# Attention and two dense blocks in one kernel: the first x block split during attention, and two units of the first dense block formed around the last head

## The chip, the cores and the metric

One core of one Trainium2 chip runs the whole program. The metric is the device time of one execution in microseconds (us), from the first to the last instruction and what the runtime puts around them. Of the kernel before three runs were taken; the median counts.

## What is computed

The reference does three things in a row, all in float32. Attention: q, k, v of 2 batches x 8 heads x 768 tokens x 64 numbers; a query sees only the keys whose nearest centroid (of 16) is its own.

```python
scores = scale * np.matmul(q, k.transpose(0, 1, 3, 2))
scores = np.where(mask, scores, -1000000000.0)
attn = np.exp(scores - scores.max(-1, keepdims=True))
attn = attn / (attn.sum(-1, keepdims=True) + 1e-09)
out = np.matmul(attn, v)          # the 8 heads side by side: x, 1536 tokens x 512
```

First dense block, with a rational gate on each number of h:

```python
h = x @ w_in                      # 512 -> 2048
g = (a[0] + a[1]*h + a[2]*h**2 + a[3]*h**3) / (1 + abs(b[0])*abs(h) + abs(b[1])*h**2 + 1e-6)
y = g @ w_out                     # 2048 -> 512
```

Second dense block: h2 = y @ w_in2 (512 to 1024), SoLU (h2 times its softmax), a layer norm, and a product with w_out2 (1024 to 512).

## The kernel before

**Attention.** The main loop (L652) goes through 96 units: head n of 16, and in it a tile t of 128 queries. For one unit, `unit_scores` (L382) forms 128 x 768 scores on PE in a pair of PSUM banks (two such pairs, tag "s", go round), `unit_max` (L399) takes the row maximum on DVE (L401), and `unit_exp` (L407) the exponential on ACT (L414). Two units make a pair; `turn_p` (L424) turns the 128 x 1536 numbers of a pair in 32 x 32 blocks on DVE (L431), one pair behind the scores. When a head is turned, `pv_step` (L434) multiplies with V on PE (L441) into four banks ("pv"), spread over the units of the next head; `pv_out` (L449) copies them out on ACT (L457, two copies: u and w). Once in two heads `pair_sums` (L463) inverts the row sums, and `pair_fin` (L498) adds u and w (L502) and scales them by the inverse sums (L516) into x. x lies in three blocks of 512 tokens, XF[0] to XF[2]; its four quarters kt are the four pairs of heads of a batch. XF[0] belongs to the first batch, which is heads 0 to 7.

**The seam.** After the loop (L688 to L706) comes, in program order: the copies of head 14's product, the turn of head 15's last pair, the sums of the last pair of heads (inverse L467, spread out by a DVE copy `rw` at L472, turned by six PE transposes into a bank pair `rbp`, L475), head 15's product with V, its two copies, `split_x(0)`, and the last `pair_fin` (on DVE). `split_x` (L635) makes of a block of x a rounded part XH (ACT, L342) and the remainder XL (POOL, L638), four quarters each: the products with float32 weights are made of three products of rounded parts (xh with wh, xl with wh, xh with wl).

**First dense block.** 48 units, one per (block of x, 128 columns of w_in). `ff_h` (L741) forms h of a unit by 12 matmuls (L752) in one of four single banks. The gate: `ff_g1` (ACT L765 t, L766 y; POOL L767 and L768 the denominator q; DVE L769, L770), `ff_g2` (ACT L776 log and L777 exponential, written over h in its bank; DVE L779 to L781, which end with the gated y), `ff_g3` (ACT L786 rounded part gh; POOL L787 remainder gl). `ff_y` (L792) multiplies with w_out by 12 matmuls (L804) into two bank pairs of tag "s". The h of a unit is formed three units ahead of its y. Beside that the weights of later units are loaded (L121, by SP) and cut into parts in the background (ACT L138, L141, L149; DVE L145; POOL L150).

The program is written as calls; a scheduler of the framework sets each engine's order from its own estimate of times, and `behind` (L527) forces one instruction behind another. Each engine then runs its own queue in order and waits on semaphores.

## Time and profile before

| | us |
|---|---|
| median of 3 runs (668.08 to 671.21) | 668.9 |
| the profiled execution | 670.29 |
| its span, first to last instruction | 668.5 |
| busy in it: PE | 608.6 |
| DVE | 507.4 |
| ACT | 436.2 |
| POOL | 375.8 |

The mean granted clock of TensorE is 0.969 of full speed. PE is the tensor engine's matmuls, PEld its weight loads, DVE the vector engine, ACT the scalar engine, POOL GpSimd, SP the engine that issues most DMAs. The busy times overlap: an engine with a high share need not be the one that sets the time at every place. Attention fills the span up to about 233 us, the first dense block most of the time up to about 533 us.

### The profile page before, as it was taken

The page shows a single profiled execution, that of the slowest core. Times are in us where ns is not written, and L with a number is a line of the kernel's source. Part 1 is how long each engine was busy: PE and PEld are TensorE (multiplying, and loading weights), DVE is VectorE, ACT ScalarE, POOL GpSimd, SP SyncE. Part 2 cuts the span into 40 slices and gives each one's busy share as a digit, 9 for nine tenths or more (in the row PEclk, how much of TensorE's full clock was granted, in tenths as well). Part 3 has the DMA queues.
Part 4 walks back from the last instruction along what each step waited for, and adds up shares of the span by engine and source line. Part 5 has one row for each costly group of instructions (what it writes and reads, how often), then busy time and mean ns, then how long its engine had stood idle before and what let it go on. Part 6 is the DMA issues. An engine that isn't in the chain of part 4 may idle for free.

```text
span 668.5 us, 13805 instructions
## 1 busy us (share of the span) xinstructions
PE 608.6 (91%) x5517; PEld 473.7 (71%) x5517; DVE 507.4 (76%) x656; ACT 436.2 (65%) x796; POOL 375.8 (56%) x347
## 2 busy tenths in 40 slices
PE   7687978888878867999999999998999999999998
PEld 3565656555655556888878888876888888888887
DVE  4789999999999737887897878899899655444360
ACT  2456666765787638979889879798685444434341
POOL 8555677656889337988798989676566100000000
PEclk8589899998999988999999999999999999999999
DMA  8966676777673204222221323223000000000001
GB/s 228 273 186 167 144 223 185 179 198 183 171 189 92 54 19 171 96 66 92 96 95 64 95 64 95 67 91 88 9 0 1 0 18 17 16 32 17 31 17 47
DMA packets 22439, 64.71 MB, mean 97 GB/s; under 512 B 4532, under 2 KB 5640, under 8 KB 22376
## 3 DMA queue, kind: packets, MB, share of 16 engines
q1 hardware_dynamic: 21944, 63.67, 33.7%
q8 instruction: 43, 0.70, 0.5%
q10 hardware_dynamic: 432, 0.17, 0.1%
q14 instruction: 20, 0.16, 0.1%
HBM read 59.16 MB, written 3.19 MB: 93 GB/s over the span
## 4 chain that ended last, share of the span: by engine, by line
PE 37%; DVE 11%; ACT 7%; issue 5%; POOL 4%; DMA 0%; DVEq 0%; ACTq 0%; SPq 0%; POOLq 0%
PE hh L895 10%; PE o L946 10%; PE y L804 8%; PE h L752 6%; DVE q L779 2%; PE lt L928 2%; DVE h L780 2%; DVE xhl L638 2%; DVE y L769 1%; POOL q L768 1%; DVE y L770 1%; ACT y L766 1%; POOL gl L787 1%; ACT h L776 1%; POOL q L767 1%
## 5 line engine op out<-in xcount | busy, mean ns | idle before, releaser
L752 PE MATMUL h<-xhl,w1h 128*128 128x512 f32 x384 | 123.7, 396 | 7.8 <-DVE y L781 5.4
L414 ACT ACTIVATE p<-s,m 128x768 f32<-128x768 f32 x96 | 86.0, 897 | 58.0 <-DVE m L401 57.8
L401 DVE TENSOR_REDUCE m<-s 128x1 f32<-128x768 f32 x96 | 88.5, 934 | 15.4 <-PE s L396 15.1
L441 PE MATMUL pv<-pt,v 32*64 32x192 f32 x3072 | 84.4, 339 | 9.6 <-ACT w L457 6.6
L752 PEld LDWEIGHTS h<-xhl,w1h 128*128 128x128 f32 x384 | 72.8, 190 | 25.5 <-DVE y L781 6.5
L431 DVE STREAM_TRANSPOSE pt<-p 128x1536 f32<-128x1536 f32 x48 | 84.5, 1762 | 0.0
L787 POOL TENSOR_TENSOR gl<-y,gh 128x512 fp32r<-128x512 f32 x48 | 69.9, 1458 | 24.4 <-ACT gh L786 24.3
L390 PE MATMUL s<-k,q 128*128 128x384 f32 x192 | 62.7, 411 | 21.6 <-ACT p L414 20.8
L441 PEld LDWEIGHTS pv<-pt,v 32*64 32x64 f32 x3072 | 57.3, 134 | 30.4 <-issue 16.1
L804 PE MATMUL y<-gl,w1h 128*128 128x512 f32 x192 | 76.0, 396 | 0.8 <-POOL gl L787 0.6
L804 PE MATMUL y<-gh,w1l 128*128 128x512 f32 x192 | 75.7, 394 | 0.0
L752 PE MATMUL h<-xhl,w1l 128*128 128x512 f32 x192 | 75.7, 395 | 0.0
L804 PE MATMUL y<-gh,w1h 128*128 128x512 f32 x192 | 70.6, 394 | 0.0
L768 POOL TENSOR_TENSOR q<-q,t 128x512 f32<-128x512 f32 x48 | 65.5, 1365 | 3.1
L390 PEld LDWEIGHTS s<-k,q 128*128 128x128 f32 x192 | 31.1, 203 | 49.0 <-ACT p L414 27.0
L767 POOL TENSOR_SCALAR q<-t,ab 128x512 f32<-128x512 f32 x48 | 40.6, 845 | 38.5 <-ACT t L765 19.4
L396 PE MATMUL s<-k,q 128*128 128x384 f32 x192 | 52.4, 357 | 2.3 <-DVE k L601 2.3
L769 DVE TENSOR_TENSOR y<-y,h 128x512 f32<-128x512 f32 x48 | 32.8, 683 | 25.9 <-ACT y L766 25.8
L776 ACT ACTIVATE h<-q,qc 128x512 f32<-128x512 f32 x48 | 33.2, 691 | 23.2 <-DVE y L770 13.2
L895 PE MATMUL hh<-vh,xhl 128*128 128x512 f32 x160 | 44.9, 396 | 0.0
L804 PEld LDWEIGHTS y<-gl,w1h 128*128 128x128 f32 x192 | 36.5, 190 | 9.8 <-POOL gl L787 1.9
L804 PEld LDWEIGHTS y<-gh,w1h 128*128 128x128 f32 x192 | 36.2, 189 | 8.5 <-ACT gh L786 0.6
(160 smaller groups left out, 1338.3 us busy)
## 6 DMA issues: line engine op xcount, KB each, us to landing
raww<-in_w SPq DMA_DIRECT2D x32, 512.0 KB, 4.0
v<-in_v SPq DMA_DIRECT2D x64, 192.0 KB, 4.9
dup<-in_qT SPq DMA_DIRECT2D x31, 192.0 KB, 3.7
dup<-in_kT SPq DMA_DIRECT2D x31, 192.0 KB, 3.8
rawv<-in_w2i SPq DMA_DIRECT2D x8, 512.0 KB, 3.6
rawv<-in_w2o SPq DMA_DIRECT2D x8, 512.0 KB, 3.6
out<-ob SPq DMA_DIRECT2D x11, 256.0 KB, 2.0
pr<-in_qT SPq DMA_DIRECT2D x7, 384.0 KB, 3.9
```

What stands on the lines that cost most here:

```text
L390: r = nc.tensor.matmul(sp[:, a, 0:384], lhsT=q1[i][:, sl], rhs=k1[i][:, a * 384:(a + 1) * 384], start=True, stop=False)
L396: last["pe"] = nc.tensor.matmul(sp[:, a, 0:384], lhsT=q2[i][:, sl], rhs=k2[i][:, a * 384:(a + 1) * 384], start=False, stop=True)
L401: last["dve"] = nc.vector.tensor_reduce(m, sp[:, :, 0:384], axis=AX.XY, op=ALU.min)
L414: last["act"] = nc.scalar.activation(out=P[n, t // 2][:, t % 2], in_=sp[:, :, 0:384], func=AF.Exp, scale=-1.0, bias=m, accum_out=rs[key][: ...
L431: r = nc.vector.transpose(PT[n][:, 2 * i:2 * i + 2].rearrange("p t k -> p (t k)"), p.rearrange("p t a k -> p (t a k)"))
L441: last["pv"] = nc.tensor.matmul(pv[n][64 * c:64 * c + 64, r, 0:192].rearrange("p (t q) -> p t q", t=NT), lhsT=vv[n][sl, j], rhs=PT[n][sl, ...
L752: r = nc.tensor.matmul(hp, lhsT=w[:, kt * 128:(kt + 1) * 128], rhs=x[:, kt], start=(i == 0), stop=(i == 11))
L768: nc.gpsimd.tensor_tensor(q, q, t, op=ALU.mult)
L787: nc.gpsimd.tensor_tensor(gl, y, gh.bitcast(F32), op=ALU.subtract)
L804: nc.tensor.matmul(o, lhsT=w[:, c], rhs=g, start=(first and i == 0), stop=(last and i == 2))
L895: last["th"] = nc.tensor.matmul(hp[:, a], lhsT=y[:, kt], rhs=w[:, 512 * a:512 * a + 512], start=(kt == 0 and e == 0), stop=(kt == 3 and e ...
L946: r = nc.tensor.matmul(op[:, 0:m], lhsT=l[:, kt], rhs=w, start=(n == 0), stop=(n == 23))
```

## The change

- `split_x(0)` is taken out of the seam and handed to the loop's plan at units 64 to 79. XHL, which held its result in the space of a turned head (tag "x"), gets a tile of its own; the space "x" is instead used by the weights of units f = 12 and 13 (`wv`).
- The pools of attention are opened in another order, with V in a pool of its own.
- `turn_p` becomes a generator. In head 15 the pair of tiles 2 and 3 is turned right after the maximum of tile 4; the last pair (tiles 4 and 5) is turned in two halves of 128 x 768.
- After the loop a bank pair of tag "s" is taken as `hb`. The h of unit 0 goes into its first bank, ahead of head 15's product with V, the h of unit 1 into its second bank, behind the six transposes to `rbp`. The transposes themselves move from ahead of head 15's product to behind it (`pair_fin`).

```diff
--- before.py
+++ after.py
@@ -104,11 +104,12 @@
     wh["l"] = ctx.enter_context(tc.tile_pool(name="wh0", bufs=1))
     asg = ExitStack()
     asp = asg.enter_context(tc.tile_pool(name="asg", bufs=1, side="right"))
+    ptp = att.enter_context(tc.tile_pool(name="ptp", bufs=1))
+    fin = att.enter_context(tc.tile_pool(name="fin", bufs=2))
+    sm = att.enter_context(tc.tile_pool(name="sm", bufs=8))
+    vp = att.enter_context(tc.tile_pool(name="vp", bufs=2))
+    pp = att.enter_context(tc.tile_pool(name="pp", bufs=2))
     qk = att.enter_context(tc.tile_pool(name="qk", bufs=2))
-    pp = att.enter_context(tc.tile_pool(name="pp", bufs=2))
-    ptp = att.enter_context(tc.tile_pool(name="ptp", bufs=1))
-    sm = att.enter_context(tc.tile_pool(name="sm", bufs=8))
-    fin = att.enter_context(tc.tile_pool(name="fin", bufs=2))
     cv[0] = att.enter_context(tc.tile_pool(name="cv", bufs=2))
 
 
@@ -159,7 +160,7 @@
 
     def w1_parts(f):
         if f in (12, 13):
-            h, l = (wv.tile([128, 1024], F32R, name=f"w1{x}{f}", tag=x) for x in "hl")
+            h, l = (wv[:, 2 * i:2 * i + 2].rearrange("p a k -> p (a k)") for i in (2 * (f - 12), 2 * (f - 12) + 1))
         else:
             h = wh["l" if f in (0, 14) else "r" if f < 5 or f == 15 else "m"].tile([128, 1024], F32R, name=f"w1h{f}", tag="h")
             l = (wl1 if NPRE < f < 12 else wl0).tile([128, 1024], F32R, name=f"w1l{f}", tag="l")
@@ -203,7 +204,7 @@
     def load_v(n):
 
         b, h = divmod(n, H)
-        t = qk.tile([128, S // 32, D], F32, name=f"v{n}", tag="v", bufs=2)
+        t = vp.tile([128, S // 32, D], F32, name=f"v{n}", tag="v", bufs=2)
         for r in range(4):
             nc.sync.dma_start(out=t[32 * r:32 * r + 32], in_=v[b, h])
         vv[n] = t
@@ -372,6 +373,8 @@
 
 
     XF = [xy.tile([128, 4, 512], F32, name=f"xf{j}", tag=f"xf{j}") for j in range(3)]
+    XHL = xy.tile([128, 8, 512], F32R, name="xhl", tag="xhl")
+    XH, XL = XHL[:, 0:4], XHL[:, 4:8]
 
     P = {}
     rs = {}
@@ -427,9 +430,14 @@
                 PT[n] = xy.tile([128, NT, S], F32, name=f"pt{n}", tag="x")
             else:
                 PT[n] = ptp.tile([128, NT, S], F32, name=f"pt{n}", tag="pt")
-        p = P.pop((n, i))
-        r = nc.vector.transpose(PT[n][:, 2 * i:2 * i + 2].rearrange("p t k -> p (t k)"), p.rearrange("p t a k -> p (t a k)"))
-        behind(r, last["dve"])
+        p = P[n, i]
+        parts = 2 if (n, i) == (B * H - 1, NT // 2 - 1) else 1
+        m = 2 // parts
+        for a in range(parts):
+            r = nc.vector.transpose(PT[n][:, 2 * i + m * a:2 * i + m * a + m].rearrange("p t k -> p (t k)"),
+                                    p[:, m * a:m * a + m].rearrange("p t a k -> p (t a k)"))
+            behind(r, last["dve"])
+            yield
 
     def pv_step(n, i):
         if i == 0:
@@ -471,9 +479,7 @@
         rw = fin.tile([128, S], F32, name="rw", tag="rb", bufs=1)
         nc.vector.tensor_copy(rw.rearrange("p (t j d) -> p j t d", t=NT, j=2), r[:, :, :, None].to_broadcast([128, 2, NT, D]))
         rb = psum2("s", "rbp")
-        for t in range(NT):
-            nc.tensor.transpose(rb[:, t // 3, t % 3 * 128:t % 3 * 128 + 128], rw[:, t * 128:t * 128 + 128], ident)
-        rsd[key] = rb
+        rsd[key] = rb, rw
 
     def sums_out(key, r, u):
 
@@ -499,6 +505,12 @@
         eng = nc.vector if key == 7 else nc.gpsimd
         b, p = divmod(key, 4)
         u, w, rb = U.pop(key), W.pop(key), rsd.pop(key)
+        if key == 7:
+            rb, rw = rb
+            for t in range(NT):
+                r = nc.tensor.transpose(rb[:, t // 3, t % 3 * 128:t % 3 * 128 + 128], rw[:, t * 128:t * 128 + 128], ident)
+                if t == 0:
+                    behind(r, last["pv"])
         eng.tensor_tensor(u, u, w, op=ALU.add)
         yield
         t0 = b * S
@@ -638,6 +650,7 @@
             el.tensor_tensor(XL[:, kt], XF[j][:, kt], XH[:, kt].bitcast(F32), op=ALU.subtract)
             yield
 
+    spread(split_x(0, nc.scalar, nc.gpsimd), 5, 64, 79)
     set1_a()
     def pv_part(n, t):
 
@@ -665,8 +678,16 @@
             load_v(n)
         sp = unit_scores(n, t)
         m = unit_max(n, t, sp)
-        if t % 2 and idx > 1:
-            turn_p(*divmod(idx // 2 - 1, NT // 2))
+        if n == B * H - 1 and t >= NT - 2:
+            if t == NT - 2:
+                for _ in turn_p(n, NT // 2 - 2):
+                    pass
+            else:
+                end = turn_p(n, NT // 2 - 1)
+                next(end)
+        elif t % 2 and idx > 1:
+            for _ in turn_p(*divmod(idx // 2 - 1, NT // 2)):
+                pass
         if idx == S1B:
             set1_b()
 
@@ -687,16 +708,27 @@
         run_plan(idx)
     for i in range(2):
         pv_out(B * H - 2, i)
-    turn_p(B * H - 1, NT // 2 - 1)
+    for _ in end:
+        pass
+    hb = psum2("s", "h01")
+
+    def h_of(hp, j, f, u):
+        w_h, w_l = w1_t[f]
+        i = 0
+        for kt in range(4):
+            for w, x in ((w_h, XH), (w_h, XL), (w_l, XH)):
+                r = nc.tensor.matmul(hp, lhsT=w[:, kt * 128:(kt + 1) * 128], rhs=x[:, kt], start=(i == 0), stop=(i == 11))
+                if i == 0 and 0 < u < 4:
+                    behind(r, last["pv"])
+                i += 1
+        return hp
+
+    h_of(hb[:, 0], 0, 0, 0)
     pair_sums(B * H // 2 - 1)
     for i in range(NS):
         pv_step(B * H - 1, i)
     for i in range(2):
         pv_out(B * H - 1, i)
-    XHL = xy.tile([128, 9, 512], F32R, name="xhl", tag="x")
-    XH, XL = XHL[:, 0:4], XHL[:, 4:8]
-    for _ in split_x(0, nc.scalar, nc.gpsimd):
-        pass
     for _ in pair_fin(B * H // 2 - 1):
         pass
     for _ in range(3):
@@ -713,7 +745,6 @@
     wh["m"] = ctx.enter_context(tc.tile_pool(name="wh1", bufs=7))
     ypp = ctx.enter_context(tc.tile_pool(name="ypp", bufs=1))
     YP = [ypp.tile([128, 4, 512], F32, name=f"yp{j}", tag=f"yp{j}") for j in range(2)]
-    wv = ctx.enter_context(tc.tile_pool(name="wv", bufs=2))
     m1 = ExitStack()
     cv[0] = m1.enter_context(tc.tile_pool(name="cv1", bufs=3))
     cw = m1.enter_context(tc.tile_pool(name="cw", bufs=2))
@@ -725,6 +756,7 @@
     nc.vector.memset(qc, 1.0 + 1e-6)
     a0, a1, a2, a3 = (coef_t[:, i:i + 1] for i in range(4))
     ff_units = [(j, f) for j in (0, 1, 2) for f in range(8)] + [(j, f) for j in (2, 1, 0) for f in range(8, 16)]
+    wv = xy.tile([128, 9, 512], F32R, name="wv", tag="x")
     bg = [w1_parts(f) for f in range(NPRE, 14)]
 
     def run_bg(k):
@@ -736,24 +768,15 @@
                 bg.pop(0)
 
     gt = {}
-    hb = [None]
 
     def ff_h(u):
         j, f = ff_units[u]
-        xh, xl = XH, XL
-        w_h, w_l = w1_t[f]
         if u and u % 8 == 0 and (f == 0 or j < 2):
             for _ in split_x(j, nc.scalar, nc.vector):
                 pass
-        hp = psum1(f"h{u}")
-        i = 0
-        for kt in range(4):
-            for w, x in ((w_h, xh), (w_h, xl), (w_l, xh)):
-                r = nc.tensor.matmul(hp, lhsT=w[:, kt * 128:(kt + 1) * 128], rhs=x[:, kt], start=(i == 0), stop=(i == 11))
-                if u < 4 and i == 0:
-                    behind(r, last["pv"])
-                i += 1
-        return hp
+        if u == 0:
+            return hb[:, 0]
+        return h_of(hb[:, 1] if u == 1 else psum1(f"h{u}"), j, f, u)
 
     live = {}
 
```

PE's queue at the seam, before (`pv14`, `pv15`: products of heads 14 and 15; `h0`: the h of unit 0):

```order
L396 MATMUL s15_5_3243<-k21_159,q21_157 128x384 x2
L441 MATMUL pv14_3166<-pt14_2997,v14_2985 64x192 x32
L475 MATMUL rbp_3294<-cst_70,rw_3292 128x128 x6
L441 MATMUL pv15_3301<-pt15_3164,v15_3152 64x192 x96
L752 MATMUL h0_3466<-xhl_3400,w1h0_2502 128x512 x2
L752 MATMUL h0_3466<-xhl_3400,w1l0_2503 128x512
```

PE's queue at the same place now (`h01` holds the h of units 0 and 1; w1h0 and w1l0 are the weights of unit 0, w1h1 of unit 1):

```order
L399 MATMUL s15_5_3256<-k21_162,q21_160 128x384 x2
L449 MATMUL pv14_3178<-pt14_3009,v14_2997 64x192 x32
L720 MATMUL h01_3303<-xhl_168,w1h0_2512 128x512 x2
L720 MATMUL h01_3303<-xhl_168,w1l0_2513 128x512
...
L449 MATMUL pv15_3321<-pt15_3176,v15_3164 64x192 x96
L511 MATMUL rbp_3320<-cst_70,rw_3318 128x128 x6
L720 MATMUL h01_3303<-xhl_168,w1h1_2648 128x512 x2
```

The 12 matmuls of unit 0 stand between the products of heads 14 and 15, and the transposes stand behind head 15's product.

ACT's queue at the seam, before:

```order
L457 ACTIVATE u7_3285<-pv14_3166 64x4x6x32
L457 ACTIVATE w7_3286<-pv14_3166 64x4x6x32
L342 ACTIVATE xhl_3400<-xf0_162 128x512 x4
L457 ACTIVATE u7_3285<-pv15_3301 64x4x6x32
L457 ACTIVATE w7_3286<-pv15_3301 64x4x6x32
L765 ACTIVATE t0_3479<-h0_3466 128x512
```

and now (`raww150` is a piece of a weight just loaded, `w1w50` and `w1h5` what is made of it):

```order
L465 ACTIVATE w7_3299<-pv14_3178 64x4x6x32
L788 ACTIVATE t0_3482<-h01_3303 128x512
L789 ACTIVATE y0_3484<-h01_3303,coef_72 128x512
L139 ACTIVATE w1w50_3493<-raww150_3476 128x512
L142 ACTIVATE raww150_3476<-raww150_3476,less_81 128x512
L799 ACTIVATE h01_3303<-q0_3483,qc_3469 128x512
L800 ACTIVATE h01_3303<-h01_3303 128x512
L809 ACTIVATE gh0_3525<-y0_3484 128x512
L465 ACTIVATE u7_3298<-pv15_3321 64x4x6x32
L465 ACTIVATE w7_3299<-pv15_3321 64x4x6x32
L150 ACTIVATE w1h5_3491<-w1w50_3493 128x512
L788 ACTIVATE t1_3516<-h01_3303 128x512
```

The four roundings of x are gone from here, and ACT's whole part of unit 0's gate stands ahead of the copies of head 15's product.

The roundings now stand in ACT's queue in heads 3, 5, 7 and 9, one in each; the second of them, in head 5:

```order
L465 ACTIVATE u1_968<-pv3_1037 64x4x6x32
L465 ACTIVATE w1_969<-pv3_1037 64x4x6x32
L417 ACTIVATE p5_2_1211,rs2_938<-s5_2_1202,m5_2_1207 128x768
L343 ACTIVATE xhl_168<-xf0_165 128x512
L417 ACTIVATE p5_2_1211,rs2_938<-s5_3_1227,m5_3_1232 128x768
```

The rounding of a quarter of XF[0] stands between the exponentials of tiles 2 and 3; the remainder on POOL stands directly behind the scalings that write XF, ahead of the next head's preparation.

## Rows read from the trace of the kernel before

**Rows 1.** The page, first part: engine, busy us (share of span), instructions.

```profile
PE 608.6 (91%) x5517; PEld 473.7 (71%) x5517; DVE 507.4 (76%) x656; ACT 436.2 (65%) x796; POOL 375.8 (56%) x347
```

**Rows 2.** Waits of PE from 232 us on: total us, times, longest us.

```profile
PE h L752 <- DVE y L781: 5.4, 2, 3.5
PE rbp L475 <- DVE rw L472: 4.8, 1, 4.8
PE h L752 <- ACT w L457: 1.8, 1, 1.8
```

**Rows 3.** A window: length, busy PE, PEld, DVE, ACT, POOL (instructions), PEclk, DMA share, GB/s.

```profile
300.00:320.00 20.00, 20.00 (x89) 16.33 (x88) 16.21 (x24) 19.12 (x33) 17.16 (x15) 1.00 0.33 105
```

**Rows 4.** Timeline from 231 us: start, length, engine, line, operation, count [idle, releaser].

```profile
231.35 1.56 PE L441 MATMUL pv<-pt,v 32*64 32x192 f32 x64
231.46 0.96 DVE L401 TENSOR_REDUCE m<-s 128x1 f32<-128x768 f32 x1 [1.95 <-PE s L396]
232.34 3.43 DVE L431 STREAM_TRANSPOSE pt<-p 128x1536 f32<-128x1536 f32 x2
232.46 0.90 ACT L414 ACTIVATE p<-s,m 128x768 f32<-128x768 f32 x1 [1.85 <-DVE m L401]
234.50 0.81 ACT L457 ACTIVATE w<-pv 64x768 f32<-64x768 f32 x1
235.91 5.26 POOL L638 TENSOR_TENSOR xhl<-xf,xhl 128x512 fp32r<-128x512 f32 x4 [5.96 <-ACT xhl L342]
235.97 1.62 DVE L472 COPY rw<-rs 128x768 f32<-128x768 f32 x1
237.74 1.51 PE L475 MATMUL rbp<-cst,rw 128*128 128x128 f32 x6 [4.83 <-DVE rw L472]
239.18 4.95 PE L441 MATMUL pv<-pt,v 32*64 32x192 f32 x192
```

**Rows 5.** Timeline from 246 us on, the first units of the gate.

```profile
248.26 20.74 SPq L121 DMA_DIRECT2D raww<-in_w  x7
249.53 0.62 PE L752 MATMUL h<-xhl,w1h 128*128 128x512 f32 x2
249.80 0.77 POOL L767 TENSOR_SCALAR q<-t,ab 128x512 f32<-128x512 f32 x1 [8.64 <-ACT t L765]
250.66 1.29 POOL L768 TENSOR_TENSOR q<-q,t 128x512 f32<-128x512 f32 x1
252.30 0.62 PE L752 MATMUL h<-xhl,w1h 128*128 128x512 f32 x2
255.09 0.71 ACT L776 ACTIVATE h<-q,qc 128x512 f32<-128x512 f32 x1
260.06 0.74 DVE L781 SCALAR_TENSOR_TENSOR y<-y,coef,h 128x512 f32<-128x512 f32 x1
260.86 0.83 PE L752 MATMUL h<-xhl,w1h 128*128 128x512 f32 x2 [3.54 <-DVE y L781]
261.83 1.75 POOL L150 TENSOR_TENSOR w1l<-w1w,w1h 128x512 fp32r<-128x512 f32 x1
265.30 0.62 PE L804 MATMUL y<-gh,w1h 128*128 128x512 f32 x2
```

**Rows 6.** Windows at 237.5 and at 468 us.

```profile
237.50:238.00 0.50, 0.26 (x2) 0.29 (x3) 0.09 (x1) 0.00 (x0) 0.50 (x1) 0.50 0.00 0
468.00:472.00 4.00, 4.00 (x16) 3.26 (x15) 4.00 (x6) 1.72 (x3) 1.50 (x1) 0.80 0.07 29
```

**Rows 7.** Timeline at 463 us, the return to the first x block.

```profile
463.02 0.50 PE L752 MATMUL h<-xhl,w1h 128*128 128x512 f32 x1 [0.65 <-ACT xhl L342]
466.11 0.78 PE L752 MATMUL h<-xhl,w1h 128*128 128x512 f32 x1 [1.83 <-DVE y L781]
```

**Rows 8.** Timeline of ACT and POOL in head 5.

```profile
94.54 2.28 POOL L516 TENSOR_TENSOR xf<-u,rb 128x512 f32<-128x512 f32 x2
95.91 0.90 ACT L414 ACTIVATE p<-s,m 128x768 f32<-128x768 f32 x1 [2.40 <-DVE m L401]
```

## The prediction

> **What bounds the kernel now.** I read the page's busy shares first: PE is busy for 608.6 of 668.5 us [rows 1], so only what keeps PE waiting or slow can be won. Next a window of the first dense block: PE fills it, 20.00 of 20 us, with ACT at 19.12 [rows 3], so nothing is to be won there. In attention the chain goes through DVE: ACT's exponential waits for its maximum, 2.40 in one unit of head 5 [rows 8]. Then PE's waits from 232 us on, for the seam between the two: 4.8 us for the copy `rw` on DVE, 1.8 us for ACT's copies, 5.4 us in two waits (the longer 3.5) for the last DVE step of a gate [rows 2]. Last the timeline of the seam [rows 4, 5].
>
> The seam begins where the last product of head 14 ends, 231.35 + 1.56 = 232.91 [rows 4], and ends where unit 0's y starts on PE, 265.30 [rows 5]: 32.4 us. The PE work in it is five units' h, head 15's product and six transposes. A unit's h takes 252.30 - 249.53 = 2.77 [rows 5]; the product has 192 matmuls, three times the 64 of 1.56 [rows 4], 4.7; the transposes took 1.51 [rows 4] at a granted clock of 0.50 [rows 6], so 0.75 at full clock. Together 5 x 2.77 + 4.7 + 0.75 = 19.3. So **13.1 us** of the seam are waits and half speed: 4.8 + 1.8 + 3.5 are the waits, the rest is mostly the half clock after the two long ones (the h that began at 260.86 took 4.44 instead of 2.77, so 1.7 [rows 5]; the transposes 0.75; the start of head 15's product).
>
> **The change, part by part.**
>
> *The split out of the seam.* Four ACT roundings and four POOL remainders go; the remainders ran 5.26 us from 235.91 [rows 4] and ended at 241.2, while the first h waited until 245.93 for the copies [rows 2]: POOL was not the last to come, so removing it gains nothing by itself. It makes the next part possible. In attention the same eight instructions come back, one of each in heads 3, 5, 7, 9. There ACT waits for POOL's scalings: in head 5 those began at 94.54 and took 2.28 for 768 columns [rows 8], so the first 512 end near 96.1; the rounding (2.17 / 4 = 0.54 [rows 4]) puts the next exponential at 96.7 where it began at 95.91 [rows 8], 0.8 late. That exponential had itself waited 2.40 for DVE's maximum [rows 8], and DVE has a transpose of 1.7 (3.43 for two [rows 4]) between: I take 0, and 0 to 1.1 us as bounds. A gain is excluded, since nothing is taken from attention.
>
> *Unit 0's h in a bank pair of the scores.* It needs only tile 4's exponential of head 15 out of its bank, done before 232 us (tile 5's began at 232.46 [rows 4]). So it runs at 232.9 to 235.7, where PE waited for `rw`. The 4.8 us wait is covered by 2.8 us of useful work.
>
> *Halves and the early pair.* The pair of tiles 2 and 3 moves into DVE's idle 1.95 us ahead of the last maximum (231.46 [rows 4]). Then the two halves, 0.9 each (half of 3.43 / 2 [rows 4]): the first after the maximum, to 233.3; the second after the last exponential, which ends at 232.46 + 0.90 = 233.36 [rows 4], so to 234.3. ACT's copy w of head 14, which frees the four banks, ends at 234.50 + 0.81 = 235.3 [rows 4]. Head 15's product starts right behind the h, 235.7, and ends at 240.4; the transposes, behind it now, at 241.1; `rw` is ready 1.62 and a short inverse after the halves [rows 4], near 236.1.
>
> *What is late next.* Unit 1's h goes into the other half of the same tile, and the program as built makes it wait for the whole gate of unit 0. That chain: ACT 0.7, POOL 0.77 and 1.29, two ACT passes of 0.7, three DVE passes of 0.74 [rows 5], 6.4 us from 235.7: 242.1. So PE waits **1.0** there. Behind that gate on ACT's queue stand the rounding gh and the copies of head 15's product, 0.7 + 2 x 0.8 [rows 4, 5], to 244.4; unit 2's h, which needs these copies, is due at 242.1 + 2.77 = 244.9, so no wait. On DVE the sum of u and w and the scalings of x follow, 768 columns each, about 1 us each (the maximum of 768 took 0.96 [rows 4]): to 246.5. ACT waits for it (a background rounding stands there whose space comes free with it), and it needs twenty passes from there to the rounding gh of unit 1. At 0.58 each, 19.12 us for 33 in the steady stretch [rows 3], that is 258.1; at the unoverlapped 0.68 of the passes in [rows 4, 5] it is 260.1. I take the second, since ACT will also wait for POOL and DVE between. POOL's remainder takes 1.3 to 1.75 more [rows 5], so 261.6. PE would be there after four h (h2 to h5), two half units of y and two matmuls: 244.9 + 4 x 2.77 + 2.77 + 0.45 = 259.1. So PE waits **2.5** for unit 1's gate; from then on the gates are ahead as they are now.
>
> *The raw loads.* Their issue moves from 248.26 [rows 5] to about 231.6, since their space is no longer freed by the last scalings. They are then done before ACT asks for them; nothing queued behind them on SP is due early. Cost 0. The new order of pools moves only who waits for whose space; I found no later wait that it adds.
>
> **Sum.** Of 13.1 us, 1.0 + 2.5 stay: gain 9.6. POOL's and DVE's passes stretch when more of them overlap: a POOL pass of 1.29 took 1.75 at 261.83 [rows 5]. Four such passes are on the new path, 0 to 1.8; I take 0.9. Gain **8.7**; the bounds are 11.6 (ACT at its fast pace, no stretch) and 6.7 (full stretch and 1.1 in attention). The profiled execution stands 1.4 above the median of its runs: 670.3 - 8.7 = 661.6 there, **660.2** as a median, with 657.3 to 662.2 from these bounds. A measurement of this kernel can tell about 0.5%, 3.3 us, from no change.
>
> **The clock, row against rule.** At 463.02 PE had waited 0.65, at 466.11 it waited 1.83 [rows 7], and the granted clock from 468 to 472 was 0.80 [rows 6]: two short waits and some work between them were followed by the half clock. The new waits of 1.0 and 2.5 are of that kind. "TensorE: Matmul & The Clock Gate" of the Trainium skill (its summary of practical rules) says to avoid long idle gaps between bursts of matmuls; by that rule the split waits here would cost only themselves, where [rows 7] would put one more stretch at half clock behind them. The rows show that short waits close together can do it.
>
> **Rivals.**
>
> *Half clock behind the new waits.* For it: [rows 7]. Against it: 15 us of unbroken work lie between the wait of 1.0 and the others. Price: as at 260.86, 1.7. Time 661.9.
>
> *ACT sets the pace.* At 19.12 of 20 us [rows 3] it has 4% to spare, and the waits that fall away were time in which it worked ahead on background weights. If half the gain comes back as small waits for gates and weights in the first 18 units: 660.2 + 4.3 = 664.5. Against it: PE showed 20.00 in that same stretch, so it can be fed.
>
> *Given back later.* The weights of units 12 and 13 and the order of the whole block are laid out anew. If a place like that at 463 us (0.65 and 1.83 [rows 7], and about 1.7 for the half clock behind them, 4 in all) comes twice more, the gain is gone: 660.2 + 8.4 = 668.6, no change. Nothing in the queues speaks for it.
>
> *Slower: the split delays attention.* ACT waits in order for POOL's scalings and POOL waits in order for ACT's rounding, in four heads where DVE's chain sets the time [rows 8]. What ACT loses is 2.40 at most where it had that slack [rows 8]; POOL inherits it, then 0.54 for the rounding and 1.3 for its own remainder (5.26 / 4 [rows 4]): up to 4.2 us by which the next head's k and q come late, in each of four heads. It decides from 3.0 us a head on (12.0 in all eat the gain and 3.3 more); between 3.0 and 4.2, at 3.6, the time is 660.2 + 14.4 = 674.6. Against it: the next head's k and q are due several units later, and the remainder stands ahead of only two or three passes that prepare them.
>
> *It does not do what it says.* It is described as a split in the last heads and two h's around the last product. In the queues the split stands in heads 3 to 9, and unit 1's h does not fill a gap, because it waits for unit 0's gate. Both are in the sum; without the second, 1.0 more would be won.
>
> **How the numbers follow.** My forecast 0.55; half clock behind the new waits 0.17; ACT sets the pace 0.12; given back later 0.09; slower 0.07. Faster by over 0.5% are the first three, 0.84; within 0.5% is 0.09; slower 0.07. The range, 656.8 to 666.5, holds the first three cases with their bounds and a small part of the fourth; outside are the slower case, most of the fourth and a remainder of the first, under 0.2 together.
>
> **What would show it.** Right: no PE wait for `rw`; 12 matmuls of h right behind head 14's product, then head 15's product without a gap; one wait of about 1 us for the last DVE step of unit 0's gate, none for the copies of head 15; unit 0's y before unit 4's h; about 2.5 us of waits for unit 1's gate in two or three pieces; then an unbroken PE, with the seam 9 us shorter and attention as long as before (its last product ending within 1 us of 232.9). Wrong: a granted clock of half speed in the 10 us behind those waits (the first rival); PE waits spread over 280 to 400 us (the second); waits above 3 us anywhere after 460 (the third); the end of attention 3 us a head later (the fourth).

## The result: 663.4 us, and the profile after

The changed kernel took 663.37 us in the median of 6 runs (661.31 to 666.46), the kernel before on the same chip 670.63 (6 runs): a ratio of 0.990, 95% interval 0.9867 to 0.9933, which is 4.5 to 8.9 us. On another chip the ratio was 0.9884 (0.9843 to 0.9924). The profiled execution took 664.1, its span is 662.3. The forecast was 660.2, which is 8.7 us under the 668.9 that three runs of the kernel before had given.

The page of the changed kernel, beside [rows 1]:

```profile
PE 606.8 (92%) x5517; PEld 472.0 (71%) x5517; DVE 504.0 (76%) x657; ACT 437.2 (66%) x796; POOL 375.7 (57%) x347
```

PE runs the same 5517 matmuls. Of the 6.2 us that the span lost, 1.8 are busy time of PE and 4.4 its idle time. PE's waits from 225 to 300 us, where [rows 2] had 4.8 for the spread inverse sums, 1.8 for the copies and 3.5 for a gate:

```profile
PE y L827 <- POOL gl L810: 1.5, 1, 1.5
PE pv L449 <- DMA v<-in_v: 1.2, 1, 1.2
PE h L720 <- DVE y L804: 0.7, 1, 0.7
PE pv L449 <- issue: 0.5, 1, 0.5
...
PE y L827 <- DVE y L804: 0.2, 1, 0.2
```

The wait for `rw` and the wait for the copies are gone. What stays is the wait of unit 1's h for unit 0's gate (0.7) and two waits of y (1.5 for unit 1's remainder, 0.2 for a gate's last DVE step). The timeline of the seam, beside [rows 4, 5]:

```profile
234.26 1.56 PE L449 MATMUL pv<-pt,v 32*64 32x192 f32 x64
...
235.74 0.73 PE L720 MATMUL h<-xhl,w1h 128*128 128x512 f32 x2
...
237.71 0.56 DVE L480 COPY rw<-rs 128x768 f32<-128x768 f32 x1
...
238.69 3.49 PE L449 MATMUL pv<-pt,v 32*64 32x192 f32 x155
...
242.63 1.19 PE L449 MATMUL pv<-pt,v 32*64 32x192 f32 x37 [0.45 <-issue]
...
243.76 0.87 PE L511 MATMUL rbp<-cst,rw 128*128 128x128 f32 x6
...
244.55 0.75 DVE L804 SCALAR_TENSOR_TENSOR y<-y,coef,h 128x512 f32<-128x512 f32 x1
...
245.33 0.63 ACT L809 ACTIVATE gh<-y 128x512 fp32r<-128x512 f32 x1 [2.35 <-DVE y L804]
...
245.35 0.73 PE L720 MATMUL h<-xhl,w1h 128*128 128x512 f32 x2 [0.72 <-DVE y L804]
...
246.81 0.80 ACT L465 ACTIVATE w<-pv 64x768 f32<-64x768 f32 x1
...
249.95 0.63 ACT L150 ACTIVATE w1h<-w1w 128x512 fp32r<-128x512 f32 x1 [2.34 <-issue]
...
262.15 0.61 ACT L809 ACTIVATE gh<-y 128x512 fp32r<-128x512 f32 x1
...
263.70 1.27 POOL L810 TENSOR_TENSOR gl<-y,gh 128x512 fp32r<-128x512 f32 x1
...
265.02 0.50 PE L827 MATMUL y<-gl,w1h 128*128 128x512 f32 x1 [1.47 <-POOL gl L810]
```

Unit 0's h starts as head 14's product ends; head 15's product follows it, and the transposes follow that. Head 15's product itself stood 0.45 us (at 242.63), and the profile shows nothing that it waited for. Two things are late. Head 14's product ends at 235.82 instead of 232.91, so 2.9 us were lost ahead of the seam. And ACT stands 2.34 us at 249.95.

How much the seam gave is read where both kernels have done the same work, at the last y of the first dense block. The view of that line, before and changed (the last start is behind "to"):

```profile
L804 PE MATMUL y<-gh,w1l x40: 389/389/398, 483.7 to 532.7; 128*128 128x512 f32 x40
```

```profile
L827 PE MATMUL y<-gh,w1l x28: 389/389/397, 480.0 to 526.5; 128*128 128x512 f32 x28
```

With 0.39 for that matmul, head 14's product to the end of the block took 533.1 - 232.9 = 300.2 us before and 526.9 - 235.8 = 291.1 now: **9.1 us less**. What comes behind took 135.4 us in both, and in all the experiments. Of the kernel before there is one profile, with three stretches at half clock in it, so the 9.1 is a difference of two single executions; the table below has more of the changed seam.

Where the 2.9 us went is read from the starts of the 96 exponentials. The last one of head 1 started 1.9 us later than before (47.29 and 45.36). The change's own instructions come later, but its order of pools is in force there: the two profiles with the old order have 44.9 and 45.4, the twelve with the new one 44.2 to 50.0, so it is not shown whether the order has a part in that. In head 2 1.4 us came on, with the granted clock at 0.89 of full speed instead of 1.00. The view of head 2, before and changed (PEclk is the third number from the end):

```profile
45.36:58.89 13.53, 10.54 (x225) 7.37 (x217) 12.93 (x14) 7.79 (x17) 8.11 (x7) 1.00 0.66 181
```

```profile
47.29:62.24 14.95, 11.94 (x225) 8.15 (x217) 12.93 (x14) 7.79 (x16) 8.37 (x7) 0.89 0.66 183
```

Three of the experiments have 0.89 and 15.0 us there too; all the others have 1.00 and the 13.5 us of the kernel before. Heads 3 and 6 added 0.45 and 0.2, heads 10, 14 and 15 gave back 0.8, 0.3 and 0.4; head 10 goes with the clock as well (0.94 of full speed before, 1.00 now). Head 5 is the change's own. Two exponentials of it before (the second is in [rows 8]) and now:

```profile
92.52 0.90 ACT L414 ACTIVATE p<-s,m 128x768 f32<-128x768 f32 x1
95.91 0.90 ACT L414 ACTIVATE p<-s,m 128x768 f32<-128x768 f32 x1 [2.40 <-DVE m L401]
```

```profile
96.31 0.90 ACT L417 ACTIVATE p<-s,m 128x768 f32<-128x768 f32 x1
...
98.33 2.28 POOL L528 TENSOR_TENSOR xf<-u,rb 128x512 f32<-128x512 f32 x2
...
99.96 0.63 ACT L343 ACTIVATE xhl<-xf 128x512 fp32r<-128x512 f32 x1 [2.67 <-POOL xf L528]
100.50 0.88 ACT L417 ACTIVATE p<-s,m 128x768 f32<-128x768 f32 x1
```

The exponential, which began 3.39 us behind the one ahead of it before, begins 4.19 behind it: 0.80 late. 0.57 of that is still there at the end of the head (14.28 us before from the end of head 4, now 14.85), in every kernel with the rounding at this place.

### The profile page after: what moved, and what is told of

Same layout as the page of the kernel before. It is cut to its first block, busy times and chain, and to the rows that moved or that the text cites. A ratio compares the mean times of both kernels' runs of the same rounds, so it can differ in the third digit from the quotient of the medians.

```text
span 662.3 us, 13802 instructions
## 1 busy us (share of the span) xinstructions
PE 606.8 (92%) x5517; PEld 472.0 (71%) x5517; DVE 504.0 (76%) x657; ACT 437.2 (66%) x796; POOL 375.7 (57%) x347
## 4 chain that ended last, share of the span: by engine, by line
PE 54%; ACT 3%; DVE 2%; issue 2%; POOL 1%; ACTq 0%; DVEq 0%; POOLq 0%
PE y L827 17%; PE h L720 15%; PE hh L918 10%; PE o L969 10%; PE lt L951 2%; ACT h L799 1%; DVE q L802 1%; POOL w1l L151 0%; DVE y L793 0%; ACT t L788 0%; ACT vh L867 0%; ACT y L789 0%; POOL q L791 0%; DVE y L792 0%; ACT h L800 0%
## 5 line engine op out<-in xcount | busy, mean ns | idle before, releaser
L720 PE MATMUL h<-xhl,w1h 128*128 128x512 f32 x336 | 106.8, 394 | 3.2 <-DVE y L804 2.5
L404 DVE TENSOR_REDUCE m<-s 128x1 f32<-128x768 f32 x96 | 88.4, 933 | 15.7 <-PE s L399 15.2
L437 DVE STREAM_TRANSPOSE pt<-p 128x1536 f32<-128x1536 f32 (+1 forms) x49 | 84.7, 1729 | 0.2 <-ACT p L417 0.2
L720 PEld LDWEIGHTS h<-xhl,w1h 128*128 128x128 f32 x336 | 63.3, 189 | 18.4 <-DVE y L804 3.2
L393 PEld LDWEIGHTS s<-k,q 128*128 128x128 f32 x192 | 31.0, 202 | 51.5 <-ACT p L417 30.3
L827 PE MATMUL y<-gl,w1h 128*128 128x512 f32 x168 | 66.3, 395 | 1.5 <-POOL gl L810 1.5
L827 PE MATMUL y<-gh,w1l 128*128 128x512 f32 x168 | 66.5, 396 | 0.0
L720 PE MATMUL h<-xhl,w1l 128*128 128x512 f32 x168 | 65.7, 392 | 0.0
L827 PE MATMUL y<-gh,w1h 128*128 128x512 f32 x168 | 61.9, 394 | 0.3 <-DVE y L804 0.2
L790 POOL TENSOR_SCALAR q<-t,ab 128x512 f32<-128x512 f32 x48 | 43.1, 898 | 31.3 <-ACT t L788 15.3
L918 PE MATMUL hh<-vh,xhl 128*128 128x512 f32 x160 | 44.9, 396 | 0.0
L802 DVE SCALAR_TENSOR_TENSOR q<-q,h 128x512 f32<-128x512 f32 x48 | 32.7, 681 | 14.2 <-ACT h L800 11.9
L399 PEld LDWEIGHTS s<-k,q 128*128 128x128 f32 x192 | 37.0, 200 | 2.4 <-issue 2.4
```

What stands on the lines that cost most here:

```text
L393: r = nc.tensor.matmul(sp[:, a, 0:384], lhsT=q1[i][:, sl], rhs=k1[i][:, a * 384:(a + 1) * 384], start=True, stop=False)
L399: last["pe"] = nc.tensor.matmul(sp[:, a, 0:384], lhsT=q2[i][:, sl], rhs=k2[i][:, a * 384:(a + 1) * 384], start=False, stop=True)
L404: last["dve"] = nc.vector.tensor_reduce(m, sp[:, :, 0:384], axis=AX.XY, op=ALU.min)
L437: r = nc.vector.transpose(PT[n][:, 2 * i + m * a:2 * i + m * a + m].rearrange("p t k -> p (t k)"), p[:, m * a:m * a + m].rearrange("p t a ...
L720: r = nc.tensor.matmul(hp, lhsT=w[:, kt * 128:(kt + 1) * 128], rhs=x[:, kt], start=(i == 0), stop=(i == 11))
L827: nc.tensor.matmul(o, lhsT=w[:, c], rhs=g, start=(first and i == 0), stop=(last and i == 2))
```

## The experiments

Each kernel was compared with the kernel before on its own chip. From each profile stand the exponentials of a head ("head 5" is from the last one of head 4 to its last) and "the seam", the 300.2 and 291.1 us above.

The last column has the windows of 5 us in the seam, by their start, in which the granted clock was under full speed; in each of them TensorE spent a part or all of the time at half clock, the lower of its two levels (1.2 GHz).

| kernel | ratio to before (95%) | head 5 | seam | windows under full clock |
|---|---|---|---|---|
| before | 1 | 14.28 | 300.2 | 235, 240, 260, 465 |
| changed | 0.990 (0.9867 to 0.9933) | 14.85 | 291.1 | 265, 460 |
| changed, again | 0.9884 (0.9843 to 0.9924) | 14.83 | 290.7 | 455, 460 |
| whole turn | 0.985 (0.9818 to 0.9882) | 14.85 | 289.3 | none |
| unit 1 in its own bank | 0.9891 (0.9854 to 0.9928) | 14.85 | 291.6 | 245, 250 |
| split only | 0.9968 (0.9943 to 0.9993) | 14.84 | 298.6 | 240, 465, 470 |
| split late | 0.9871 (0.984 to 0.9902) | 14.28 | 289.3 | none |
| coefficients late | 0.987 (0.9834 to 0.9905) | 14.83 | 289.3 | none |
| split behind last exponential | 0.9879 (0.9838 to 0.992) | 14.28 | 289.2 | none |
| y's pool first | 0.9841 (0.9801 to 0.9881) | 14.83 | 288.8 | 460 |
| both | 0.9836 (0.9795 to 0.9876) | 14.28 | 289.8 | 450, 455, 460 |
| both, copies ahead of gh | 0.9824 (0.978 to 0.9868) | 14.28 | 288.0 | 455 |
| old pools | 0.9975 (0.9949 to 1.0) | 14.84 | 297.7 | 260, 265, 270 |
| split behind the sums | 0.978 (0.9752 to 0.9808) | 14.28 | 286.5 | none |

**The changed kernel again.**

> The changed kernel itself, on the same chip as the next three, so that they have it beside them. Theory: 0.985 to 0.99 of the kernel before, as in its first comparison. From the end of head 14's product to the end of the first dense block it was 291.07 us; the changed kernel with the four roundings moved to later heads, the same program from there on, took 289.32, with no stretch at half clock behind the wait for unit 1's gate. If that half clock comes in some executions only, this one shows 289 to 290 or 291 to 292. Rival: 291.1 belongs to the changed kernel and the late roundings changed something behind them too.

Its seam took 290.7. Windows of the changed kernel:

```profile
265.00:270.00 5.00, 4.98 (x15) 3.95 (x16) 4.26 (x6) 4.26 (x8) 5.00 (x5) 0.66 0.10 30
...
460.00:465.00 5.00, 5.00 (x15) 3.96 (x16) 5.00 (x6) 3.52 (x6) 3.28 (x2) 0.66 0.34 105
```

and of this second profile of it:

```profile
265.00:270.00 5.00, 5.00 (x23) 4.09 (x22) 3.91 (x6) 4.24 (x8) 5.00 (x5) 1.00 0.14 32
...
460.00:465.00 5.00, 5.00 (x19) 3.96 (x18) 5.00 (x5) 2.89 (x5) 2.67 (x2) 0.75 0.24 93
```

The same program falls to half clock behind unit 1's wait in one profile and not in the other. The stretch near 460 costs 290.7 - 289.3 = 1.4; the one at 265 only 0.3, since PE would have waited later instead: the second profile has a wait of 0.85 for a remainder at 288.12, the first has none there. Seams are compared below with this in mind.

**Transposes of head 15 as before.**

```diff
-        if n == B * H - 1 and t >= NT - 2:
...
-        elif t % 2 and idx > 1:
+        if t % 2 and idx > 1:
...
-        parts = 2 if (n, i) == (B * H - 1, NT // 2 - 1) else 1
+        parts = 1
```

> The changed kernel with head 15's transposes as they were before: the pair of tiles 2 and 3 is turned after the last maximum and the last pair in one piece. Theory: the halves are worth little, 0 to 0.5 us, because the product of head 15 now stands behind the 2.8 us of unit 0's h and behind ACT's copies of head 14 (it began at 238.69 in the changed kernel, while the two whole transposes would be done about 3.5 us after the last maximum, near 239.0). Rival: the transposes are on the path, and without the halves the product and all behind it come 1.7 to 3.4 us later. Decides: the start of head 15's product after the last product of head 14 (2.87 us in the changed kernel).

The seam took 289.3, as in the three profiles of the changed seam without half clock (289.2 to 289.3). The product waited 0.17 and began 3.1 us behind head 14's product, not 2.87:

```profile
240.58 3.49 PE L449 MATMUL pv<-pt,v 32*64 32x192 f32 x155 [0.17 <-DVE rs L475]
```

The halves are worth 0.2 us there, and nothing at the end of the block.

**Unit 1's h in a bank of its own.**

```diff
-        return h_of(hb[:, 1] if u == 1 else psum1(f"h{u}"), j, f, u)
+        return h_of(psum1(f"h{u}"), j, f, u)
...
-    turn[0] += turn[0] % 2
+    turn[0] += turn[0] % 2 + 1
```

The second pair of lines starts the second dense block one step further in the round of banks; what comes behind the seam took 135.4 us as ever.

> The changed kernel with unit 1's h in one of the four single banks, as before, instead of the second bank beside unit 0. Theory: it must then wait for ACT's copies of head 15's product, which stand behind unit 0's whole gate on ACT (done at 247.6 in the changed kernel, where the h began at 245.35): PE idle 2 to 3 us more behind the transposes, 2 to 3 us slower in all. Rival: since unit 1's h waits for unit 0's gate anyway, its place does not matter: within 0.7 us of the changed kernel.

The scheduler put half of unit 0's y ahead of that h, so PE stood for unit 0's gate in full:

```profile
PE y L827 <- POOL gl L810: 1.9, 3, 0.9
PE y L827 <- ACT gh L809: 1.4, 1, 1.4
```

and the clock fell behind it. 291.6 is 2.3 us over the changed seam without half clock, as the theory had it, though through y and not through the copies; the total (0.9891) can't tell it from the changed kernel.

**The split alone.**

```diff
-    hb = psum2("s", "h01")
...
-    h_of(hb[:, 0], 0, 0, 0)
...
+        for t in range(NT):
+            nc.tensor.transpose(rb[:, t // 3, t % 3 * 128:t % 3 * 128 + 128], rw[:, t * 128:t * 128 + 128], ident)
+        rsd[key] = rb
```

Head 15's transposes are as before, too, and all h lie in the single banks.

> Of the change only the split in attention, the own tile for it and the order of pools; the transposes, the six PE transposes and the first two units' h stand at the seam as in the kernel before. Theory: the gain is made by the h that fills PE's wait, so this alone gains 1 to 2 us of the seam's 9 (PE's wait for the spread inverse sums shrinks by the shorter copy on DVE, 1.62 to about 0.6, since POOL is idle beside it). Rival: taking 2.2 us off ACT and 5.3 us off POOL at the seam, and the loads that start 14 us earlier, make half of the gain or more: 4 us or more.

The seam is 1.6 us shorter, the time 0.3% (2.1 us), as the theory had it. The waits of before are all there. The first is 3.76 instead of 4.83, by a shorter copy, the second is the same 1.8, and the third, for the gate, is 1.58 instead of 3.54, with two of 0.5 and 0.6 for remainders behind it. The granted clock fell for longer near 465 than before, so the 1.6 is not the copy alone.

```profile
239.59 0.56 DVE L480 COPY rw<-rs 128x768 f32<-128x768 f32 x1
240.29 1.01 PE L483 MATMUL rbp<-cst,rw 128*128 128x128 f32 x6 [3.76 <-DVE rw L480]
```

So most of the 9.1 us needs what this run leaves out: the h in the scores' banks, with the six transposes moved behind head 15's product. No run separates these two.

**Attention's pools as before.**

```diff
+    qk = att.enter_context(tc.tile_pool(name="qk", bufs=2))
+    vp = qk
+    pp = att.enter_context(tc.tile_pool(name="pp", bufs=2))
     ptp = att.enter_context(tc.tile_pool(name="ptp", bufs=1))
-    fin = att.enter_context(tc.tile_pool(name="fin", bufs=2))
     sm = att.enter_context(tc.tile_pool(name="sm", bufs=8))
...
+    fin = att.enter_context(tc.tile_pool(name="fin", bufs=2))
```

> The changed kernel with attention's pools opened in the order of the kernel before. The first temporary of the gate then lies where u and w lay, so on ACT unit 0's gate stands behind the copies of head 15's product and waits for DVE's last scaling, and the first raw loads wait for it as well, as before. Theory: the early h of unit 0 is then worth little: its gate begins near 248 to 250 instead of 238.8, unit 1's h waits for all of it, and 5 to 8 us of the 9 won at the seam are lost. Rival: the order of pools only moves loads that are in time anyway: within 1 us of the changed kernel.

The seam took 297.7: of the 9.1 us 2.5 are left. Unit 0's gate began at 246.62, behind the copies of head 15's product and 0.2 us behind the end of DVE's last scaling, whose space, by the layout of the pools, its first temporary needs, and PE stood once for 8.4 us. It stood not at unit 1's h, as the theory had it: PE ran the h of five units without a wait between (244.25 to 258.3), and the wait came in unit 0's y.

```profile
246.62 0.60 ACT L788 ACTIVATE t<-h 128x512 f32<-128x512 f32 x1 [2.41 <-issue]
```

```profile
PE y L827 <- DVE y L804: 8.4, 1, 8.4
```

The granted clock was low for longer in one stretch than in any other seam (0.86, 0.50 and 0.62 in the windows from 260), so the loss is of wait and clock together. The part of the change that looks like bookkeeping decides whether the early h is of use.

**The split in heads 10 to 12.**

```diff
-            rnd(eh, XH[:, kt], XF[j][:, kt])
+            if j == 0 and eh is nc.scalar and el is nc.gpsimd:
+                behind(eh.activation(out=XH[:, kt], in_=XF[j][:, kt], func=AF.Copy, scale=1.0), last["act"])
```

> The changed kernel with the four roundings forced behind the exponentials of units 64, 67, 71 and 75 (heads 10 to 12), where x has long been written. Theory: in heads 3 and 5 of the changed kernel ACT and POOL meet scalings that are not finished (in head 5 ACT stood 2.67 us for POOL and the next exponential came 0.8 us later than before, and the delay stayed), so attention gets 0.8 to 1.6 us shorter. Rival: the four roundings and remainders cost the same wherever they stand, or the delays are drift from the start of the run: attention within 0.4 us of the changed kernel when counted from head 2 on.

Head 5 is as before the change (14.28), but heads 11 and 12 took 12.33 and 14.92 instead of 10.81 and 13.14: 3.3 us for 0.6. ACT has background weights to convert there, and is full. With a rounding added it reaches its pass over the row sums late, and DVE stands 1.92 us for it, where the kernel before has 1.34:

```profile
184.05 0.89 ACT L417 ACTIVATE p<-s,m 128x768 f32<-128x768 f32 x1
184.93 0.69 ACT L139 ACTIVATE w1f<-raww 128x512 f32<-128x512 f32 x1
...
187.01 0.23 DVE L475 RECIPROCAL rs<-rs 128x12 f32<-128x12 f32 x1 [1.92 <-ACT rs L474]
```

That is 0.6 of the 3.3; 2.0 came at the last exponential of head 12, and how the rounding leads to it was not followed. The theory named the right wait in head 5, and its cure was dearer than the illness. By this profile the change would have lost more, had the split stood in the late heads, as the plan in the code says; the times (0.9871) can't tell.

**The split behind the last exponential of its head** (units 23, 35, 47, 59; pinned as above).

> The changed kernel with each of the four roundings forced behind the exponential of the last tile of its head (heads 3, 5, 7, 9), after POOL's scalings have written that quarter of x. Theory: ACT no longer stands for POOL, and heads 5, 7 and 9 take what they took before (tile 2 to tile 5 of head 5: 7.73 us instead of 8.30): attention 0.8 us shorter than in the changed kernel. Rival: the instruction costs its 0.6 us on ACT wherever it stands, as it did in heads 11 and 12, where it cost 1.5 and 1.8: no gain or a loss.

The rival held. Head 5 lost its delay, but heads 6, 8 and 10 each began 0.51 us later, by the same path: the rounding stands ahead of the pass over the sums, and DVE's inverse waits for that.

```profile
101.19 0.63 ACT L650 ACTIVATE xhl<-xf 128x512 fp32r<-128x512 f32 x1
...
102.96 0.29 ACT L474 ACTIVATE rs<-rs,tiny 128x12 f32<-128x12 f32 x1
104.36 0.90 ACT L417 ACTIVATE p<-s,m 128x768 f32<-128x768 f32 x1 [1.11 <-DVE m L404]
```

The last row shows a place that should cost nothing: behind the sums ACT is idle for 1.1 us.

**One ACT instruction out of the start.**

```diff
-    nc.scalar.activation(out=ab, in_=coef_t[:, 4:6], func=AF.Abs)
+    behind(nc.scalar.activation(out=ab, in_=coef_t[:, 4:6], func=AF.Abs), last["act"])
```

> The changed kernel with one small ACT instruction, the absolute value of two coefficients for the gate, forced behind the last exponential; it stands in ACT's queue between the first two exponentials and waits there for its DMA, 1.36 us in the profile of before, 3.39 in that of the changed kernel, 0.66 to 4.16 in the others. Theory: the start of the program is on the path and this wait is most of what differs between executions there: 1 to 3 us faster than the changed kernel, and the runs nearer to each other. Rival: the wait is taken up by the head that follows (DVE and PE behind it have other work): within 0.7 us.

This is nearer to the rival. The first two exponentials are 0.9 us apart instead of 1.1 to 5.3, but the last of head 1 began at 46.7, where the other profiles have 44.2 to 50.0. The ratio, 0.987, can't be told from the changed kernel's 0.9884 on the same chip.

**The pool of y first.**

```diff
-    wh["m"] = ctx.enter_context(tc.tile_pool(name="wh1", bufs=7))
     ypp = ctx.enter_context(tc.tile_pool(name="ypp", bufs=1))
+    wh["m"] = ctx.enter_context(tc.tile_pool(name="wh1", bufs=7))
```

> The changed kernel with the pool of the partial sums y opened ahead of the pool of the converted weights, so that the first background rounding at the seam no longer lies in the space of u, w and the spread inverse sums and does not wait on ACT for DVE's last scaling. Theory: ACT waits there 2.34 us in the changed kernel with all of unit 1's gate queued behind; without it the gate comes 2.3 us earlier, PE's wait for unit 1's remainder (1.47) goes, and with it the half clock behind it (where it comes): 1.5 to 3.2 us faster between the end of head 14's product and the end of the first dense block. Rival: ACT is full there, the gate is paced by its 20 passes and not by that wait: less than 0.7.

The seam took 288.8 with one half-clock stretch, 1.9 us under the changed kernel's 290.7 with one, as the theory had it. ACT's background rounding follows the copies without a wait (beside 249.95 above), and PE's waits for remainders fell from 2.3 us (in the changed kernel's second profile) to 1.1:

```profile
249.70 0.81 ACT L465 ACTIVATE w<-pv 64x768 f32<-64x768 f32 x1
250.53 0.63 ACT L150 ACTIVATE w1h<-w1w 128x512 fp32r<-128x512 f32 x1
```

```profile
PE y L827 <- POOL gl L810: 1.1, 2, 0.9
```

**Both.**

> Both gains together: the roundings pinned behind the last exponential of their heads, and the partial sums' pool opened first. Theory: they lie in different places (heads 5 to 9, and 12 to 30 us behind head 14's product) and add up: from tile 5 of head 1 to tile 5 of head 14 about 173.4 us (changed kernel 174.7 and 174.9), from head 14's product to the end of the first dense block 287.3 where PE keeps its clock and 288.8 where it falls once near 460 us; 2.5 to 3 us faster than the changed kernel, 0.980 to 0.985 of the kernel before. Rival: attention is followed by a seam that waits for something else, and what comes earlier waits longer: within 1 us of the changed kernel.

**Both, with the copies of head 15's product ahead of gh.**

> The kernel with both gains, and on ACT unit 0's rounding gh behind the two copies of head 15's product instead of ahead of them: ACT stood 2.35 us for DVE there with the copies queued behind. Theory: the copies come 2 us earlier, but unit 1's gate begins with its h on PE, which is not earlier, so 0 to 0.5 us are won. Rival: the copies lead to the last scalings and to everything that waits for their space, so 1.5 us or more are won.

0.9836 and 0.9824 against 0.9841 for the pool alone: the pinned roundings add nothing that these runs can tell, as their own run said. With both, the seam came to 289.8, 1.0 over what was expected for one fall of the clock: the clock was at 0.50 for the whole of 455 to 460 and low on either side. From tile 5 of head 1 to tile 5 of head 14 it was 175.0 instead of 173.4, 1.5 of it in head 2, at a granted clock of 0.89. The seam with the copies ahead is 288.0 with one half-clock stretch, against 288.8 for the pool alone with one: 0.8 us, a little over what was expected.

**The split behind the sums, with both of the above.**

```diff
+                behind(eh.activation(out=XH[:, kt], in_=XF[j][:, kt], func=AF.Copy, scale=1.0), last["rs"])
...
+        plan[NT * (2 * kt + 4)].append(early_x)
```

> The kernel with the partial sums' pool first and the copies ahead of gh, and each of the four roundings one step further back: behind ACT's small pass over the row sums at the start of heads 4, 6, 8 and 10, not behind the last exponential. Behind the last exponential each of them delayed that pass, DVE's inverse waited for it (1.40 us at head 6), and the first exponential of heads 6, 8 and 10 came 0.51 later than before. Theory: ACT is idle for 1.1 us there, between the sums and the next maximum, so a rounding of 0.6 costs nothing: from head 5 to head 9 as before the change (heads 5, 6, 7, 8: 14.28, 14.15, 11.79, 13.07), 0.6 us less than the changed kernel and 1 to 1.5 less than with the roundings behind the last exponential. Rival: POOL's remainder, now between the preparations of the next head, delays k and q and some scores: the same 0.5 a head, or more.

```profile
107.12 0.33 ACT L474 ACTIVATE rs<-rs,tiny 128x12 f32<-128x12 f32 x1
107.32 0.65 ACT L650 ACTIVATE xhl<-xf 128x512 fp32r<-128x512 f32 x1
```

Heads 5 to 8 took 14.28, 14.37, 11.79 and 13.06: 0.2 us over the kernel before in all. The time is 659.64 us (658.11 to 660.53), 0.978 of before. Its interval lies below both of the changed kernel's, so this version is faster than the changed kernel.

## Why the prediction was right

**The direction and the seam.** The forecast said 13.1 us of waits and half speed, of which 3.5 stay: 9.6, less 0.9 for stretched passes. The seam gave 9.1 with half clock twice and 10.9 (300.2 - 289.3) without. The steps, each against the end of head 14's product (forecast, then measured): head 15's product starts 2.8 / 2.87; unit 0's gate ends 9.2 / 9.5; the copies end 11.5 / 11.8; DVE's scalings free ACT 13.6 / 14.1; unit 1's gh ends 27.2 / 26.9; its remainder 28.7 / 29.2. PE's waits were 1.0 and 2.5 / 0.7 and 1.8. The choice between ACT's two paces came out for the reason given, not by the pace: the twenty passes took 12.8 us, between the 11.6 at 0.58 and the 13.6 at 0.68, and the 12.8 are a pace of 0.58 and one wait of 1.17 for POOL (at 254.11). The gate's end, 0.3 late, and the free space, 0.5 late, were made up there. The 0.9 for stretched passes was an allowance; no run measures it by itself. Half clock three times in the one profile before and twice in the one now belongs to the 9.1 too.

**Attention: the step that failed.** "That exponential had itself waited 2.40 for DVE's maximum ...: I take 0." 0.8 late was right, the cover was not: the exponential ended its wait when the maximum came, so it was on the chain with nothing to spare. 0.57 stayed, and the changed kernel's heads 7 and 9, with a rounding each, took what they had taken (within 0.05). In head 3, which has the first, the clock hides the cost: in all 14 profiles it took 13.5 us at full granted clock, 14.0 to 14.6 at 0.88, and 15.2 to 15.3 at 0.78 to 0.80. The bound of 1.1 held for heads 5 to 9 together, which took 0.8 more than before. The slower rival named this wait (ACT stood 2.67 us for POOL), at a far higher price; the 3.3 us in the late heads came another way. The sign "its last product ending within 1 us of 232.9" failed: it ended 2.9 later, mostly by the start and by the clock in head 2.

**"The new order of pools moves only who waits for whose space; I found no later wait that it adds."** It added none at the seam, but the sum gave the order no value, and it has one: without it 6.6 us of the seam's gain go.

**The clock.** The first rival came in the changed kernel's profile (0.66 behind unit 1's wait), and cost 0.3, not 1.7. In four other profiles with the same seam the same wait was followed by full clock. ACT as the pace maker: PE is busy for 20.00 of 20 us in each window from 280 to 440, so no.

**The size.** A gain of 8.7 was forecast, 7.3 was measured between the medians, and 8.7 lies at the upper edge of the interval. Of the 3.2 us between the forecast 660.2 and the measured 663.4, 1.7 is the kernel before, whose six runs have a median of 670.6 and not 668.9. The kernels with the changed seam and the split in heads 3 to 9 at that place came to 0.990, 0.9884 and, with parts that proved worth nothing, 0.985 and 0.987. Most of the scatter between the profiles lies at the start: the last exponential of head 1 came between 44.2 and 50.0 us. Next come heads 2 and 3, with the clock. So the total says less of the change than the seam does. That 9.1 came so near 8.7 is in part luck: PE's two waits were 1.0 us shorter than forecast, and the 0.45 at head 15's product and the half clock at 265 (0.3) took most of that back.

## What to carry to other kernels

A wait in the profile says what came last, not that there is time to spare: an instruction that waited 2.4 us and starts the moment its input is there passes on a delay beyond it (0.57 of 0.80 us in head 5). To hide work on a full in-order engine, look for where it is idle *behind* the instructions that others wait for, and pin it there. And when work is moved ahead of a seam, ask of each instruction that it brings forward whose space its output takes.

## What was not expected of the hardware

The copy `rw` took 1.62 us before [rows 4], started 0.06 us behind a POOL pass of 1.3, and 0.56 in the changed kernel and with the split alone, where POOL is idle there. "SBUF — State Buffer" of the Trainium skill (Who interferes with whom) has a DVE copy and a GpSimd instruction contend for one pair of ports where the copy runs in a mode with two ports, the second waiting for the first. By that rule an estimate from these rows is that the copy would end at 235.91 + 1.3 + 0.56 = 237.8; it ended at 237.6, so the trace agrees within 0.2 us, though it does not show the mode.

In or just behind the second of the two waits near 460 us (0.6 and 1.8, alike in 12 of the profiles) the granted clock fell in 7 and stayed full in 5, for a cost of about 1.4 us. "TensorE: Matmul & The Clock Gate" of the Trainium skill (Why this matters for your kernels) warns of long idle gaps; here two short ones near each other were followed by it, in some executions.
